# Softmax row sums and one unit's norms moved to GpSimd, and the sixth unit's loads moved behind a gather, in a fused attention and feed-forward kernel

## The chip, the cores and the metric

The kernel runs on one core of one Trainium2 chip. The metric is the time of one execution on the device in microseconds. Engines are named as the profile names them: PE (TensorE), ACT (ScalarE), DVE (VectorE), POOL (GpSimd), and SP, the queue that issues most DMAs. Each engine works through its own list of instructions in order, and an instruction that waits holds up all that stand behind it in that list.

## What is computed

The inputs are q, k and v of 8 batches, 12 heads, 448 positions and 64 values, and two weights. The reference, cut to what matters:

```python
q_n = q / (np.linalg.norm(q, axis=-1, keepdims=True) + 1e-06)
k_n = k / (np.linalg.norm(k, axis=-1, keepdims=True) + 1e-06)
scores = np.matmul(q_n, k_n.transpose(0, 1, 3, 2)) / tau
attn = np.exp(scores - np.max(scores, axis=-1, keepdims=True))
attn = attn / (np.sum(attn, axis=-1, keepdims=True) + 1e-09)
attn_out = np.matmul(attn, v)
x = attn_out.transpose(0, 2, 1, 3).reshape(B * S, H * D)   # 3584 x 768
h = x @ w_in                                                # 768 x 2048
return (h * np.cos(h)) @ w_out                              # 2048 x 768
```

## The kernel before

**Tiling.** Two heads make a pair (48 pairs, g = 0 to 47), three pairs a unit (16 units, u = 0 to 15), two units a batch. So the sixth unit is unit 5, the third is unit 2. For each unit the kernel loads q and k (`load`, L524, SP) and v (`load_v`, L536, POOL's queue); squares them (`square`, L556), sums the squares over the 64 values (`reduce`, L570, DVE) and turns the sums into 1/norm (`rnorm`, L582: ACT takes Ln and then Exp of -0.5 times it). `scale` (L594, POOL) multiplies q and k by it, and a DMA transposes the result (`transposes`, L612; the first nine pairs are transposed on PE).

**Attention of a pair.** `scores` (L640) multiplies on PE into the PSUM tiles SC, and ACT takes the exponential into PX. `attend` (L668) multiplies PX by v and by ones into the PSUM tile AV: one half of AV holds the unscaled output, the other the row sums. For the pairs in `direct` the inverse of the sum is taken at once on ACT (Ln, then Exp, L742 and L744). For the others both halves are copied to `xu`, and a chain follows once the unit is through.

**The chain** (`chain`, L755) works on units 2, 4 and on to 15: 13 chains, of 21 columns in 11 cases and 14 columns in two (units 2 and 5, where one pair is direct). Four small DMAs gather the sums over 128 partitions (L759); DVE adds two parts (L765, label "sum") and takes the reciprocal (L768, "recip"); a DMA writes it to DRAM (L769, "spread") and two read it back onto all partitions (L771, "bcast"); POOL multiplies `xu` by it into `xT` (L775). All DMAs of the chain are issued by SP.

**Feed-forward.** `m1(b)` (L778) multiplies a batch's `xT` by w_in in 8 groups on PE, with Sin on ACT and a product on DVE (L806) into `gT`; its first two groups take the batch's six chunks of `xT` one after another, in the order given, so that the last may come late. ACT has to load another function table before `m1` and again behind it (L496), and every exponential and Ln listed ahead of it in the program goes before. The product with w_out (`m2_quarters`, L850, and `m2_fill`, L878) is cut into small pieces that fill PE between the pieces of attention; DVE copies the two PSUM halves of a finished tile of 128 rows, PO and TP, to `osb` (`m2_drain`, L831, L837), and PE cannot begin the next tile in them before that.

**What sets the order.** The program is first listed as operations with costs, and `arrange` (L101) and `play` (L128) plan it: PE keeps the listed order from unit 2 on, while each other engine takes, at every free moment of a simulated run, the ready operation with the earliest due time (`late`, plus a `bias` of its own). `order_only` (L88) puts one operation behind the start of another on the same queue; in a load this is the argument `behind`. The plan's order is then written out as fixed lists, with semaphore waits. The costs in the plan are constants in the code; POOL's scale, for instance, is put at 0.1 + 896 * 1.75e-3 = 1.67 us.

**Around the change.** `pair` (L967) lists the loads of unit u+2 at L996 and of its v at L998; the loads of v of unit 4 are listed at L1044, and those of q and k of unit 5 when u is 3 (L996, without a `behind`). In the run of before SP issues the loads of unit 5 at 67 to 74 us, then an output, then the gather of unit 2.

Of the kernel before, what the change touches and what calls it, by code (L numbers as in the profile page):

```python
# [7 lines left out]
ALU = mybir.AluOpType  # L8
F32 = mybir.dt.float32
# [4 lines left out]
PLAN = {  # L14
    "apart": 1,
    "grid": {2: (16, 5, 6), 3: (11, 3, 4), 4: (8, 2, 3)},
    "hold": 0.6,
    "margin": 1.0,
    "sq": ["AA", "A", "A", "P", "P", "P"],
    "scale": ["PD", "P", "P", "P", "P", "P"],  # L20
    "second": 0,
    "mixed": (3, (0, 1, 2, 0, 1, 2, 0, 1), (2, 3, 4, 0, 1, 5)),
    "other": 8,
    "inside": 7,
# [334 lines left out]
def bass_cosine_attention__then__act_gcu_kernel(  # L359
# [13 lines left out]
    UP = 3  # L373
# [26 lines left out]
    def sb(name, shape, dt):  # L400
        return ctx.enter_context(nc.sbuf_tensor(name, shape, dt))
# [13 lines left out]
    n2 = sbs("n2", 2, [128, UH * NB], F32)  # L415
    lnn = sbs("lnn", 2, [128, UH * NB], F32)
    rn = sbs("rn", 2, [128, UH * NB], F32)
# [5 lines left out]
    RB = sbs("RB", 2, [128, UP * S], F32)  # L423
    sums = sbs("sums", 2, [128, 2 * SPR], F32)
    rcp = sbs("rcp", 2, [128, SPR], F32)
# [3 lines left out]
    zt = sb("zt", [128, S], BF16)  # L429
    ones = sb("ones", [128, 96], BF16)  # L430
    iot = cosb[0].bitcast(I32).ap()[:, 0:128]
    cst = sb("cst", [128, 2], F32)

    SC = [ps("SC%d" % i, [128, 2 * 512], F32) for i in range(2)]
    AV = ps("AV", [128, 2 * 512], F32)
# [6 lines left out]
    scr = nc.dram_tensor("scr", (NU, UH * S), F32)  # L442
# [14 lines left out]
    n2v = [t.ap().rearrange("p (h s) -> p h s", h=UH) for t in n2]  # L457
# [29 lines left out]
    def act(fn, reads, writes, cols, table=None, aps=0, label="", bias=0.0):  # L487
        o = P.op("ACT", fn, reads, writes, cost=0.165 + cols / 1200.0 + 0.09 * aps, label=label, bias=bias)
        if table is not None:
            if last_table[0] is not None:  # L490
                P.order_only(last_table[0], o)
            last_table[1].append(o)
        return o
# [9 lines left out]
    def dve(fn, reads, writes, cycles, lock=False, label="", bias=0.0):  # L503
        return P.op("DVE", fn, reads, writes, cost=0.15 + cycles / 960.0, lock=lock, label=label, bias=bias)

    def pool(fn, reads, writes, cost, label="", bias=0.0):
        return P.op("POOL", fn, reads, writes, cost=cost, lock=True, label=label, bias=bias)
# [5 lines left out]
    dve(lambda e: e.tensor_scalar(ident.ap(), iot, 0, None, ALU.is_equal), [("cos", 0)], ["ident"], 128)  # L513
    dve(lambda e: e.memset(cst.ap()[:, 0:1], math.pi / 2.0), (), ["cst0"], 1)
    dve(lambda e: e.memset(cst.ap()[:, 1:2], 1e-12), (), ["cst1"], 1)
    pool(lambda e: e.memset(ones.ap()[:, 0:64], 1.0), (), ["ones"], 0.15)
    pool(lambda e: e.memset(ones.ap()[:, 64:96], 0.0), (), ["zeros"], 0.12)
    table(EXPSET)
# [17 lines left out]
    def load_v(u, behind=None, reads=()):  # L536
        if u >= NU:
            return
        i = u % 3
        b, hb = u // 2, UH * (u % 2)  # L540
        dma("POOL", [lambda e, z=z: e.dma_start(
            vav[i][BP * z : BP * z + BP, :, 1 - z : NT3 + 2 - z, :].rearrange("p h x d -> p h (x d)"),
            bass.AP(v.tensor, (b * NH + hb) * S * D + NT3 * D * z, [[NB * D, BP], [S * D, UH], [1, (NT3 + 1) * D]]))
            for z in range(2)],
            list(reads), [("va", i)], "va%d" % i, 2.67, "load v u%d" % u, behind,
            pad=LATE if u > 1 else 0.0)
# [33 lines left out]
    rnv = [t.ap().rearrange("p (h s) -> p h s", h=UH) for t in rn]  # L580

    def rnorm(u, p0, p1, t=(0, 1)):  # L582
        i = u % 2
        h, w = slice(2 * p0, 2 * p1), slice(*blocks(t))
        n = (p1 - p0) * 2 * (w.stop - w.start)
        tag = "%d.%d" % (u, p0) + ("" if len(t) == 2 else "ab"[t[0]])
        keys = [(p, z) for p in range(p0, p1) for z in t]
        act(lambda e: e.activation(lnnv[i][:, h, w], n2v[i][:, h, w], ACT.Ln, bias=cst.ap()[:, 1:2]),
            [("n2", i, p, z) for p, z in keys] + ["cst1"], [("lnn", i, p, z) for p, z in keys],
            n, "E", 1, "ln" + tag)  # L590
        act(lambda e: e.activation(rnv[i][:, h, w], lnnv[i][:, h, w], ACT.Exp, scale=-0.5),  # L591
            [("lnn", i, p, z) for p, z in keys], [("rn", i, p, z) for p, z in keys], n, "E", 0, "rn" + tag)
# [162 lines left out]
    def chain(u):  # L755
        i, b = u % 2, u // 2
        n = sum(UP * u + p not in PLAN["direct"] for p in range(UP))
        w = SPR // UP * n
        dma("SP", [lambda e, r=r, a=a: e.dma_start(  # L759
            sums[i].ap()[64 * a : 64 * a + 64, w * r : w * r + w],  # L760
            bass.AP(xu, ((64 * a + 32 * r) * 5 + 3 + i) * UP * S, [[5 * UP * S, 1], [w, 64], [1, w]]))
            for r in range(2) for a in range(2)], [("xs", i, p) for p in range(n)], [("sums", i)], "sums%d" % i, 0.7,
            "gather%d" % u)
        r = rcp[i].ap()[:, 0:w]
        dve(lambda e: e.tensor_reduce(out=r, in_=sums[i].ap()[:, 0 : 2 * w].rearrange("p (r x) -> p x r", r=2),  # L765
                                      axis=mybir.AxisListType.X, op=ALU.add), [("sums", i)], [("rcp", i)], 2 * w,
            label="sum")
        dve(lambda e: e.reciprocal(r, r), [("rcp", i)], [("rcp", i)], 8 * w, label="recip")  # L768
        dma("SP", [lambda e: e.dma_start(bass.AP(scr, u * UH * S, [[w, 128], [1, w]]), r)],  # L769
            [("rcp", i)], [("scr", u)], "scr", 0.02, "spread%d" % u)  # L770
        dma("SP", [lambda e, a=a: e.dma_start(  # L771
            RBv[i][64 * a : 64 * a + 64, 0:n], bass.AP(scr, u * UH * S + a * n * S, [[0, 64], [1, n * S]])) for a in range(2)],
            [("scr", u)], [("RB", i, p) for p in range(n)], "RB%d" % i, 3.4 * n / UP, "bcast%d" % u, None, 2.4, 0.5)
        for p in range(n):
            pool(lambda e, p=p: e.tensor_tensor(xTv[b % 2][:, UP * i + p, :], xuv[:, u % 3, p, :], RBv[i][:, p, :], ALU.mult),  # L775
                 [("RB", i, p), ("xa", u % 3, p)], [("xT", b % 2, UP * i + p)], 1.1, label="x%d" % (UP * u + p))
# [148 lines left out]
    def find(label):  # L925
        return [o for o in P.ops if o.label == label][-1]
# [24 lines left out]
    def loads(u, behind=None):  # L951
        if u < NU:
            for p in range(UP):
                load(u, p, p + 1, behind=behind)
# [12 lines left out]
    def pair(g, f):  # L967
        u, p = g // UP, g % UP
        if 3 <= u < NU - 1:
            if p == 0:  # L970
                norms(u + 1, 0)
            if p == u % 2:
                norms(u + 1, 1)
        late = g > PB
        quarters = g >= PB
        if late and g - 1 not in points:
            attend(g - 1, direct(g - 1), (0,))
        scores(g, 0)
        m2_fill(f[0], quarters)
        if late and g - 1 in points:  # L980
            attend(g - 1, direct(g - 1), (0,))
        scores(g, 1)
        if late and f[1] and quarters:
            attend(g - 1, direct(g - 1), (1,))
            m2_fill(f[1], quarters)
            attend(g - 1, direct(g - 1), (2,))
        elif late:
            attend(g - 1, direct(g - 1), (1, 2))
        elif 1 <= g < PB:
            attend(g - 1, direct(g - 1))  # L990
        if g >= 1 and g != PB:
            if g > PB and not direct(g - 1) and (g % UP == 0 or direct(g)):
                chain((g - 1) // UP)
            if g % UP == 0:
                if g > PB and (u <= 3 or u % 2 == 0):
                    loads(u + 2, find("bcast%d" % (2 if u == 4 else u - 1)) if u > 3 else None)  # L996
                if g > PB:
                    load_v(u + 2, None if u == 5 else find("x%d" % (g - 1 if u < 5 or u % 2 == 0 else g - 4)),  # L998
                           [("sums", 0)] if u == 5 else [])
        if g == PB:  # L1000
            for y in range(PLAN["inside"], TD):
                transposes(y)
            m2_fill(f[1], True)
        if g + 2 < PB:
            norms((g + 2) // UP, (g + 2) % UP)
        if g + 1 < PB:
            transposes(g + 1, g + 1 < PLAN["apart"])
        if TD <= g + 2 < NG:
            transposes(g + 2)
        scores(g, 2)  # L1010
        m2_fill(f[2], quarters)
        scores(g, 3)
        m2_fill(f[3], quarters)
        if p == UP - 1 and u >= 3 and u % 2 == 0:
            loads(u + 3, find("bcast%d" % (u - 1)) if u > 4 else None)
# [25 lines left out]
    m1(0, 2, NKC - 1)  # L1041
    load_v(3, find("W2.3"))
    norms(3, 1)
    load_v(4, find("scale3.2"))  # L1044
    loads(4)
    P.free = False
    m2_add(0)
# [57 lines left out]
```

## Time and profile before

| | us |
|---|---|
| median of 3 runs | 442.25 |
| lowest and highest of them | 442.02 and 444.96 |
| the profiled execution, its own time | 443.33 |
| its span, first to last instruction | 441.4 |
| PE busy | 422.2 |
| ACT busy | 270.9 |
| POOL busy | 228.4 |
| DVE busy | 188.1 |

PE is busy for 96% of the span; the matmuls overlap in the records, so a busy PE is one that has work under way. The mean granted clock of PE is 0.990 of full speed. In lines of the profile, `out<-in` are the tiles written and read, brackets hold the idle time of the engine ahead of the instruction and what ended it, and "SPq" is SP's issuing of a DMA.

### The profile page before, as it was taken

What the parts mean: (1) busy time and instruction counts of PE and PEld (TensorE: products, weight loads), DVE (VectorE), ACT (ScalarE), POOL (GpSimd) and SP (SyncE); (2) the same over time, 40 slices, a digit from 0 to 9 for tenths busy, and PEclk for the clock granted to TensorE, in tenths of its full rate; (3) what the DMA queues carried; (4) which work ended last, traced back from release to release, by engine and by line L of the source; (5) the groups of instructions that cost most, each with busy time, mean ns of one, the idle gap of its engine ahead of it and who ended that gap; (6) DMA issues with size and microseconds to landing.
All of it is one profiled execution on the core that took longest, in us unless ns stands there. A gap on an engine that the chain in (4) does not pass through costs nothing.

```text
span 441.4 us, 13536 instructions
## 1 busy us (share of the span) xinstructions
PE 422.2 (96%) x6056; PEld 232.5 (53%) x6056; DVE 188.1 (43%) x243; ACT 270.9 (61%) x356; POOL 228.4 (52%) x182
## 2 busy tenths in 40 slices
PE   8889989799999999999999999999999999999996
PEld 3334545455555555664455645665556645555563
DVE  3543763425833328421772239230862244223421
ACT  4987577576688654886477855875577845703400
POOL 4999729479381566562949085924948023003000
PEclk9999999889999999999999999999999999999999
DMA  8999999999167998658927897949965940141022
GB/s 194 263 258 217 245 166 154 204 202 206 23 98 97 183 210 201 99 127 209 223 36 165 160 220 147 163 84 227 226 107 90 155 110 1 39 119 55 2 71 71
DMA packets 80713, 64.32 MB, mean 146 GB/s; under 512 B 45712, under 2 KB 75408, under 8 KB 80656
## 3 DMA queue, kind: packets, MB, share of 16 engines
q1 hardware_dynamic: 62528, 50.68, 55.8%
q0 software_dynamic: 18048, 12.59, 19.4%
q8 instruction: 47, 0.77, 0.8%
q10 hardware_dynamic: 80, 0.20, 0.1%
q14 instruction: 10, 0.08, 0.1%
HBM read 55.67 MB, written 11.14 MB: 151 GB/s over the span
## 4 chain that ended last, share of the span: by engine, by line
PE 61%; DMA 15%; POOL 11%; issue 4%; SPq 4%; ACT 2%; DVE 2%; ACTq 0%; POOLq 0%; DVEq 0%
PE SC L789 16%; PE AV L789 10%; PE TP L864 8%; PE PO L864 8%; DMA W<-in_moe_w_out_dram 7%; POOL qks L599 4%; PE SC L648 4%; PE AV L687 4%; DMA sums<-xu 3%; POOL xT L775 3%; DMA RB<-scr 3%; PE PO L894 2%; POOL sq L567 2%; PE SC L894 2%; PE TP L894 2%
## 5 line engine op out<-in xcount | busy, mean ns | idle before, releaser
L663 ACT ACTIVATE PX<-SC 128x448 bf16<-128x448 f32 (+1 forms) x192 | 153.4, 823 | 33.4 <-PE SC L648 21.6
L864 PE MATMUL PO<-W,gT 64*64 64x384 bf16 x1408 | 145.8, 328 | 4.5 <-DVE osb L837 3.3
L864 PE MATMUL TP<-W,gT 64*64 64x384 bf16 x1408 | 145.8, 328 | 0.4
L599 POOL TENSOR_TENSOR qks<-raw,rn 128x896 bf16<-128x896 f32 (+1 forms) x48 | 79.3, 1678 | 40.7 <-ACT rn L591 40.7
L789 PE MATMUL SC<-xT,W 128*128 128x448 bf16 x480 | 98.3, 352 | 0.0
L775 POOL TENSOR_TENSOR xT<-xu,RB 128x448 bf16<-128x448 f32 x37 | 41.0, 1136 | 96.9 <-DMA RB<-scr 96.9
L864 PEld LDWEIGHTS PO<-W,gT 64*64 64x64 bf16 x1408 | 77.3, 108 | 23.2 <-DVE osb L837 6.2
L864 PEld LDWEIGHTS TP<-W,gT 64*64 64x64 bf16 x1408 | 77.1, 108 | 15.9 <-PE TP L864 2.2
L567 POOL TENSOR_TENSOR sq<-raw 128x896 bf16<-128x896 f32 x45 | 75.3, 1690 | 10.7 <-DMA raw<-in_q_dram 6.3
L804 ACT ACTIVATE cosb<-SC,cst 128x896 f32<-128x896 f32 x40 | 40.1, 1006 | 54.5 <-PE SC L789 51.7
L789 PEld LDWEIGHTS SC<-xT,W 128*128 128x128 bf16 x480 | 46.7, 98 | 44.1 <-POOL xT L775 0.4
L789 PE MATMUL AV<-xT,W 128*128 128x448 bf16 x288 | 62.0, 353 | 1.9 <-POOL xT L775 1.0
L574 DVE TENSOR_REDUCE n<-sq 128x14 f32<-128x896 bf16 (+2 forms) x49 | 51.4, 1055 | 6.9 <-ACT sq L565 5.9
L806 DVE TENSOR_TENSOR gT<-SC,cosb 128x896 bf16<-128x896 f32 x40 | 43.5, 1090 | 22.3 <-ACT cosb L804 22.2
L648 PE MATMUL SC<-qkT 64*64 64x448 bf16 x576 | 52.3, 362 | 0.7 <-DVE gT L806 0.3
L804 ACT ACTIVATE cosb<-AV,cst 128x896 f32<-128x896 f32 x24 | 24.2, 1007 | 38.8 <-PE AV L789 38.8
L789 PEld LDWEIGHTS AV<-xT,W 128*128 128x128 bf16 x288 | 27.0, 98 | 31.2 <-POOL xT L775 4.4
L837 DVE COPY osb<-PO 128x384 f32<-128x384 f32 x26 | 14.4, 555 | 66.5 <-PE PO L864 60.0
L806 DVE TENSOR_TENSOR gT<-AV,cosb 128x896 bf16<-128x896 f32 x24 | 26.2, 1090 | 38.2 <-ACT cosb L804 38.1
L734 DVE COPY xu<-AV 128x896 f32<-128x896 f32 x23 | 24.9, 1083 | 39.7 <-PE AV L703 39.6
L687 PE MATMUL AV<-PX,va 128*32 128x448 bf16 x576 | 36.2, 356 | 0.0
L680 PE MATMUL AV<-PX,va 64*64 64x224 bf16 x192 | 25.9, 263 | 2.4 <-DVE xu L734 1.0
(63 smaller groups left out, 352.0 us busy)
## 6 DMA issues: line engine op xcount, KB each, us to landing
raw<-in_k_dram SPq DMA_DIRECT2D x48, 224.0 KB, 6.6
raw<-in_q_dram SPq DMA_DIRECT2D x48, 224.0 KB, 7.7
out_dram<-osb SPq DMA_DIRECT2D x55, 192.0 KB, 3.4
RB<-scr SPq DMA_DIRECT2D x22, 336.0 KB, 4.9
va<-in_v_dram POOLq DMA_DIRECT2D x32, 192.0 KB, 8.0
W<-in_moe_w_in_dram POOLq DMA_DIRECT2D x4, 768.0 KB, 14.2
W<-in_moe_w_out_dram POOLq DMA_DIRECT2D x4, 768.0 KB, 25.6
RB<-scr SPq DMA_DIRECT2D x4, 224.0 KB, 4.2
```

Of the source, the lines that this page charges most:

```text
L567: pool(lambda e, x=x, y=y: e.tensor_tensor(y, x, x, ALU.mult), src_, dst, 0.1 + n * 1.78e-3, label="sq%d.%d" % (u, p)).pad = LATE if u > 1 ...
L574: dve(lambda e, w=w: e.tensor_reduce(out=n2v[i][:, 2 * p : 2 * p + 2, w], in_=sqv[p][:, :, w, :], axis=mybir.AxisListType.X, op=ALU.add), ...
L599: f = lambda e, s0=s0, s1=s1: e.tensor_tensor(qksv[i][:, p, s0:s1].rearrange("p s h d -> p h s d"), rawv[i][:, h, s0:s1, :], bass.AP(rn[i] ...
L648: m = e.matmul(SCv[z][BP * o : BP * o + BP, a, 0:S], t[r, c - 1 + (NT3 + 1) * o, 0:BP], t[r, :, BP : 2 * BP], start=True, stop=True)
L663: act(lambda e: e.activation(PHv[j] if c == 0 else PXv[j][:, c - 1], SCv[z][:, :, 0:n], ACT.Exp, scale=1.0 / TAU), ["SC%d" % z], [("PX", j ...
L687: t = e.matmul(AVv[o : o + 32, 0, 0:S], vav[y][:, 2 * p + a, c + 1, d : d + 32], PXv[j][:, c, a, :], start=False, stop=(c == NT3 - 1))
L775: pool(lambda e, p=p: e.tensor_tensor(xTv[b % 2][:, UP * i + p, :], xuv[:, u % 3, p, :], RBv[i][:, p, :], ALU.mult), [("RB", i, p), ("xa", ...
L789: t = e.matmul(ph[:, a, 0:S], W1v[:, order[c], 128 * n : 128 * n + 128], xTv[b % 2][:, order[c], :], start=(c == 0), stop=(c == NKC - 1))
L804: act(lambda e, ph=ph, cz=cz: e.activation(cosv[cz], ph[:, :, 0:S], ACT.Sin, bias=cst.ap()[:, 0:1], scale=1.0), names(gi) + ["cst0"], [("c ...
L806: dve(lambda e, ph=ph, cz=cz, gi=gi: e.tensor_tensor(gTv[:, 2 * gi : 2 * gi + 2, S * (b % 2) : S * (b % 2) + S], ph[:, :, 0:S], cosv[cz], ...
L864: r = e.matmul(POH[b][x : x + 64, 0:HW], gTv[k, y, col + x : col + x + 64], W2v[k, y, HW * b : HW * b + HW], start=(y == 0 and h == 0), st ...
L894: r = e.matmul(po[:, 0:HW], gTv[:, y, col : col + 128], W2v[:, y, HW * hf : HW * hf + HW], start=(y == 0), stop=(y == NF - 1))
```

## The change

It does five things.

- In each of the 13 chains, the sum is a `tensor_tensor` add on POOL instead of a `tensor_reduce` on DVE, and the reciprocal is a `tensor_tensor` with the operation power and a constant -1 on POOL, instead of DVE's `reciprocal`. The plan's costs for them are 0.15 and 0.4 us.
- For unit 12 alone, 1/norm is an add of 1e-12 and a power of -0.5 on POOL (42 columns, 0.15 and 0.6 us in the plan), in place of Ln and Exp on ACT.
- The loads of q and k of unit 5 are put behind the start of unit 2's gather on SP. The spread and the broadcast of unit 2 get a bias of -8 us on their due times.
- The load of v of unit 4 is put behind the load of v of unit 3 instead of the last scaling of unit 3; that of v of unit 5 is put behind the product `x6` instead of `x8`.
- Two constants are written by DVE at the start.

```diff
+    "power": (12,),
...
-    cst = sb("cst", [128, 2], F32)
+    cst = sb("cst", [128, 4], F32)
...
+    dve(lambda e: e.memset(cst.ap()[:, 2:3], -1.0), (), ["cst2"], 1)
+    dve(lambda e: e.memset(cst.ap()[:, 3:4], -0.5), (), ["cst3"], 1)
...
+        if u in PLAN["power"]:
+            x, y = n2v[i][:, h, w].rearrange("p h s -> p (h s)"), rnv[i][:, h, w].rearrange("p h s -> p (h s)")
+            pool(lambda e: e.tensor_scalar(y, x, 1e-12, None, ALU.add), [("n2", i, p, z) for p, z in keys],
+                 [("rn", i, p, z) for p, z in keys], 0.15, label="ad" + tag)
+            pool(lambda e: e.tensor_tensor(y, y, bass.AP(cst, 3, [[4, 128], [0, n]]), ALU.pow),
+                 [("rn", i, p, z) for p, z in keys] + ["cst3"], [("rn", i, p, z) for p, z in keys], 0.6, label="pw" + tag)
+            return
...
-        dve(lambda e: e.tensor_reduce(out=r, in_=sums[i].ap()[:, 0 : 2 * w].rearrange("p (r x) -> p x r", r=2),
-                                      axis=mybir.AxisListType.X, op=ALU.add), [("sums", i)], [("rcp", i)], 2 * w,
-            label="sum")
-        dve(lambda e: e.reciprocal(r, r), [("rcp", i)], [("rcp", i)], 8 * w, label="recip")
+        parts = sums[i].ap()[:, 0 : 2 * w].rearrange("p (r x) -> p r x", r=2)
+        pool(lambda e: e.tensor_tensor(r, parts[:, 0], parts[:, 1], ALU.add), [("sums", i)], [("rcp", i)], 0.15, label="sum")
+        pool(lambda e: e.tensor_tensor(r, r, bass.AP(cst, 2, [[4, 128], [0, w]]), ALU.pow), [("rcp", i), "cst2"], [("rcp", i)], 0.4,
+             label="recip")
         dma("SP", [lambda e: e.dma_start(bass.AP(scr, u * UH * S, [[w, 128], [1, w]]), r)],
-            [("rcp", i)], [("scr", u)], "scr", 0.02, "spread%d" % u)
+            [("rcp", i)], [("scr", u)], "scr", 0.02, "spread%d" % u).bias = -8 if u == 2 else 0.0
...
-            [("scr", u)], [("RB", i, p) for p in range(n)], "RB%d" % i, 3.4 * n / UP, "bcast%d" % u, None, 2.4, 0.5)
+            [("scr", u)], [("RB", i, p) for p in range(n)], "RB%d" % i, 3.4 * n / UP, "bcast%d" % u, None, 2.4, 0.5).bias = -8 if u == 2 else 0.0
...
-                    loads(u + 2, find("bcast%d" % (2 if u == 4 else u - 1)) if u > 3 else None)
+                    loads(u + 2, find("bcast%d" % (2 if u == 4 else u - 1)) if u > 3 else find("gather2") if u == 3 else None)
...
-                    load_v(u + 2, None if u == 5 else find("x%d" % (g - 1 if u < 5 or u % 2 == 0 else g - 4)),
+                    load_v(u + 2, None if u == 5 else find("x%d" % (6 if u == 3 else g - 1 if u < 5 or u % 2 == 0 else g - 4)),
...
-    load_v(4, find("scale3.2"))
+    load_v(4, find("load v u3"))
```

## The prediction, made before the changed kernel ran

> **What bounds the kernel now.** I read the engine table of the page first, then the 40 slices, then the waits, then the timelines around the slices where PE is not full.
>
> ```profile
> PE 422.2 (96%) x6056; PEld 232.5 (53%) x6056; DVE 188.1 (43%) x243; ACT 270.9 (61%) x356; POOL 228.4 (52%) x182
> ...
> PEclk9999999889999999999999999999999999999999
> ```
>
> PE has work for 96% of the span, so a change pays only where PE is empty or slow. The 441.4 us hold 19 us without PE work, and the clock row has one hole, in slices 8 and 9 (77 to 99 us). A table by stretches takes that hole apart (columns: stretch, its length, busy time of PE, PE's weight loads, DVE, ACT and POOL with counts, granted clock, DMA share, GB/s).
>
> ```profile
> 74.00:82.11 8.11, 8.11 (x188) 4.68 (x180) 1.62 (x2) 6.20 (x10) 6.77 (x5) 1.00 1.40 190
> 82.11:85.38 3.27, 0.01 (x2) 0.00 (x1) 1.35 (x5) 1.10 (x2) 1.77 (x3) 0.86 0.94 150
> 85.38:91.30 5.92, 5.92 (x80) 3.66 (x84) 2.46 (x3) 1.98 (x4) 1.13 (x1) 0.50 0.96 188
> 91.30:98.46 7.16, 7.01 (x157) 3.72 (x149) 2.27 (x4) 5.97 (x11) 5.73 (x5) 1.00 1.09 235
> ```
>
> PE is empty for 3.27 us, and then works 5.92 us at half clock. The timeline of DVE there says why:
>
> ```profile
> 77.00 1.08 DVE L574 TENSOR_REDUCE n<-sq 128x14 f32<-128x896 bf16 x1
> 84.00 0.18 DVE L765 TENSOR_REDUCE rcp<-sums 128x14 f32<-128x28 f32 x1 [5.92 <-DMA sums<-xu]
> 84.22 0.24 DVE L768 RECIPROCAL rcp<-rcp 128x14 f32<-128x14 f32 x1
> 84.37 0.49 DVE L837 COPY osb<-PO 128x384 f32<-128x384 f32 x1
> 84.78 0.54 DVE L837 COPY osb<-TP 128x384 f32<-128x384 f32 x1
> ```
>
> DVE stands 5.92 us at the sum of unit 2, whose gather has not landed; behind it in DVE's list are the copies out of PO and TP, and without them PE cannot open the next w_out tile. PE's own waits name them, and the waits of DVE give the size of the habit:
>
> ```profile
> PE PO L864 <- DVE osb L837: 3.3, 1, 3.3
> ...
> PE AV L680 <- DVE xu L734: 1.0, 1, 1.0
> ```
>
> ```profile
> DVE rcp L765 <- DMA sums<-xu: 33.2, 10, 7.0
> ```
>
> The second PE wait is the same thing at unit 5, with AV in the place of PO: DVE waits 5.99 us and PE 1.03.
>
> ```profile
> 146.73 0.18 DVE L765 TENSOR_REDUCE rcp<-sums 128x14 f32<-128x28 f32 x1 [5.99 <-DMA sums<-xu]
> 146.94 0.24 DVE L768 RECIPROCAL rcp<-rcp 128x14 f32<-128x14 f32 x1
> 147.10 1.03 DVE L734 COPY xu<-AV 128x896 f32<-128x896 f32 x1
> ```
>
> Of the 33.2 us that DVE waits at sums, then, 4.3 reach PE; the clock adds the rest.
>
> **The change, part by part.**
>
> *Sum and reciprocal leave DVE.* DVE then holds nothing that waits for a gather. The copies of 84.37 can run when PE has finished the tile, before 82.11. Gain: 3.27 us at unit 2 and 1.03 at unit 5. The half clock follows the gap: a mean clock of 0.86 over the 3.27 us means that it fell 0.92 us before the gap's end ((1 - 0.86) * 3.27 / 0.5), 2.35 us into the idling, and nowhere else inside the span did PE idle over 2 us or its clock fall before the end. Without the gap, the 5.92 us of work at 0.50 take 2.96. Gain: 2.96 us. ACT and POOL are not full in these 5.92 us (1.98 and 1.13 us busy), so PE can run at its own speed.
>
> The Trainium skill ("TensorE: Matmul & The Clock Gate", What's actually happening) puts the fall to half clock at an idle window of about 3.4 us that runs freely. Here 2.35 us of idling were enough, so I go by the row; by the page a remaining stall of 1 to 3 us would cost itself alone, and by the row it can cost itself and as much again in slow matmuls.
>
> *They arrive on POOL.* The add: POOL's product of 448 columns takes 1.136 us and a one-column memset 0.10, so 2.3 ns a column and 0.15 us for 21 columns; at POOL's ratio to DVE on the same product (L748: 1134 against 624 ns) it would be 0.36. The power has no row on POOL. Below, it can cost no less than such an add, 0.15. ACT's Ln and Exp of 42 columns, the same function, take 0.32 and 0.24, 0.56 together. DVE's reciprocal costs 6.6 ns a column (288 against 242 ns for 21 and 14), 5.5 times its plain copy (1083 ns for 896); two such functions at POOL's 2.3 ns are 25 ns a column, 0.63 us for 21. I take 0.6, as both estimates lie there; the far end, ten times as much a column, is 5.4 us. Against DVE's 0.198 + 0.288 + 0.04 = 0.53 us, the pair on POOL takes 0.8 with a hand-over, 0.25 more.
>
> Who waits for that: the products into xT. For the first unit of a batch they have time (unit 10's broadcast lands 2 us before they start). For units 7, 9, 13 and 15 they release PE with little to spare, but the spread stands behind an output on SP there: it is issued 0.72, 0.32 and 0.70 us after the reciprocal at 7, 9 and 13, and at 15 the second broadcast chunk comes some 0.6 us ahead of PE. So 0.25 us more costs nothing; beyond about 0.6 it would cost four times the excess. POOL is idle 12 to 30 us ahead of these products (96.9 us in 9 waits), so the sum finds it free.
>
> What is queued behind POOL's new wait: at unit 5 only the products of unit 4, for which POOL waits 4.97 us anyway; at units 11 and 14 nothing (15.0 and 7.8 us idle); at units 6, 8, 10 and 12 the next unit's scaling, ahead of which POOL idles 4.4 to 6.0 us for ACT. That cover hides 13 * 0.8 = 10 us of POOL's time.
>
> *Unit 5's loads behind the gather; v of unit 4 sooner, of unit 5 later; the bias.* Before, SP issued six loads of unit 5 from 67.08 to 74.08, then an output, and the gather from 75.41, though its sums were ready at 73.24 (the copy of 72.15 + 1.09). The gather took 8.6 us to its landing behind 1.3 MB of them. On a quieter bus unit 15's took 3.8 (385.07 to the sum at 388.90) and unit 4's 5.1. So: issue near 73.5, landing near 78. The spread and broadcast took 9.5 us from 84.0 to 93.5; from 79 they end near 88.5, and the bias keeps SP's loads from stepping in. PE, 6.2 us earlier, starts the feed-forward of batch 1 at 98.46 - 6.23 = 92.2 and asks for these chunks after the 12 matmuls of the first three, at 94.5. The broadcast has 3 to 5 us in hand for its two products; no gain by itself, it keeps the 6.2 us from being lost at the next wait. If the gather stayed at 84.0, products at 93.5 to 95.8 would cost PE about 1 us.
>
> The price: unit 5's q and k come 9 us later. Its last square began at 80.89 and Exp of its norms ended at 92.65; the table load for Sin, which that Exp must precede, moves from 100.57 to 94.3. Squares from about 89, reduce 1.08 and ACT 0.56 end at 92.4. That fits by 2 us: cost nothing, but see the first rival. The v loads move 0.4 MB each between slack places: unit 4's to POOL's idle 8.6 us before 63.91, unit 5's behind x6 (needed after 120 us). Nothing.
>
> *Unit 12's norms.* POOL idles 4.40 us before 276.17 waiting for ACT's Exp, which waits for the table load (274.19 to 275.47). With add and power on POOL (0.2 and up to 1.2 us) the three scalings start some 3 us sooner. PE has no gap over 0.1 us there: nothing. The two constants, 59 ns each, lie in DVE's idle first microseconds.
>
> **The sum.** 3.27 + 2.96 + 1.03 = 7.26 us. The profiled execution took 443.33 (span 441.4 and 1.9 around it), so 436.1 by its own time. It stands 1.08 above the median of the runs, 442.25; against that median it is **435.0 us**.
>
> **The rivals.**
>
> *Unit 5 comes too late (chance 0.16).* The red and Ln of unit 5 take the place of the sum: DVE or ACT stands at them with copies or exponentials behind, between 88 and 95 us. For it: the 2 us in hand above, and that loads landed 8 us after issue on this bus (the last at the square of 80.89, issued at 72.34). Against it: v of unit 4 and of unit 5 leave this stretch. A stall of 3 us gives 438.0, and with a clock that falls again as much more, 441.0.
>
> *The wait only changes engines (0.08).* POOL stands at the gather where DVE did, and the products x8 to x11 behind it hold PE, or another copy binds PE at 82 us. For it: POOL is busy 6.77 of 8.11 us there. Against it: these products are asked for only from 92 us on, and ACT waits for PE, not PE for ACT. It would give back all of the 6.2 us: 441.2, no change.
>
> *The power is slow, and the kernel slower (0.10).* Place: the last chains of batches, units 7, 9, 13 and 15, where POOL's result releases PE. Price: four times what exceeds the 0.25 us, less some 2.3 us of slack (0.72 + 0.32 + 0.70 + 0.6). With an excess d over DVE's pair, 4d - 2.3 = 7.26 at d = 2.4, a power of 2.7 us: from there on the kernel is slower. At 5.4 us, d is 5.1 and the time 435.0 + 18 = 453. Against it: neither estimate above comes near 2.7.
>
> The Trainium skill ("GPSIMD Engine Reference", Instruction dispatch) tells of some 6 us for the first call of freshly loaded code on this engine. By that page the power of unit 2, the first, would end near 85 and its products near 96.5, 2 us after PE asks: 437 in place of 435.0. No row here shows such a load.
>
> **How the numbers follow.** The forecast has 0.66, the rivals 0.16, 0.08 and 0.10. The forecast's own range is 433.3 to 437: below if unit 7's PE gap (1.25 us with its small pieces) closes as SP's order changes, above by 2 us for the power or the gather. The range for 8 in 10 takes in the first rival: **433.3 to 441.0**. A measurement of this kernel tells about 1%, 4.4 us, from no change: faster is below 437.8. Of the forecast nearly all lies there, of the first rival little: faster 0.66. Within 1% lie the rest of the first and the second, 0.24. Slower is the power, 0.10.
>
> **What would show it.** Right: no DVE wait on sums; no PE gap near 82 and near 147 us; clock 1.00 from 6 us to the end; the first Sin of batch 1 near 96.6 in place of 102.83; the power under 1 us. The gather of unit 2 landing near 78. Wrong: a PE wait on DVE or ACT between 84 and 96, a clock below 1.00 in slices 8 and 9, PE gaps over 1 us at the xT of units 7, 9, 13 or 15, or a power of 2 us and more.

## The result, and the profile after

The changed kernel is slower: 461.28 us (median of 6 runs, 458.63 to 464.20) against 442.84 for the kernel before (6 runs, 442.02 to 444.96), a ratio of 1.041 with a 95% interval of 1.036 to 1.045. I had forecast 435.0. Here and below, times are medians of all runs of a kernel, while ratios, and the differences worked out from them, leave out the slow runs, those over 1.5% above the fastest of their kernel. The profiled execution took 458.63 us with a span of 456.6, 15.2 more than before.

The page after (busy time and share of the span; the granted clock in 40 slices):

```profile
PE 424.7 (93%) x6056; PEld 231.3 (51%) x6056; DVE 183.5 (40%) x219; ACT 270.7 (59%) x354; POOL 284.2 (62%) x210
...
PEclk9999999999999889999999999998999999999999
```

PE runs the same 6056 matmuls in a longer span, the hole in the granted clock has moved from slices 8 and 9 to slices 14 and 15 (with a smaller one in 28), and POOL has 56 us more to do. The groups of POOL by form say where that is (count, busy time, mean ns of one, idle time ahead):

```profile
L777 POOL TENSOR_TENSOR rcp<-rcp,cst 128x21 f32<-128x21 f32 x11 | 40.7, 3700 | 0.8
...
L595 POOL TENSOR_TENSOR rn<-rn,cst 128x42 f32<-128x42 f32 x1 | 7.1, 7087 | 0.1
...
L777 POOL TENSOR_TENSOR rcp<-rcp,cst 128x14 f32<-128x14 f32 x2 | 5.2, 2602 | 0.2
...
L776 POOL TENSOR_TENSOR rcp<-sums 128x21 f32<-128x21 f32 x11 | 2.4, 221 | 24.3 <-DMA sums<-xu 24.3
```

The power takes 3.70 us for 21 columns, 2.60 for 14 and 7.09 for 42: about 160 ns a column ((3.70 - 2.60) / 7 = 0.157 us and (7.09 - 3.70) / 21 = 0.161) on top of some 0.4 us. The add, at 0.22 us, is as cheap as I had it.

What the change was meant to cure is cured. The timeline of DVE around the old hole shows both copies from PO and TP at 80.6 to 81.7 us, with no sum ahead of them:

```profile
76.48 0.62 DVE L757 COPY xu<-AV 128x448 f32<-128x448 f32 x1 [3.21 <-PE AV L697]
80.63 0.56 DVE L847 COPY osb<-PO 128x384 f32<-128x384 f32 x1 [3.52 <-PE PO L874]
81.10 0.55 DVE L847 COPY osb<-TP 128x384 f32<-128x384 f32 x1
```

The stretches of the changed kernel (same columns as in the prediction) show PE full and at clock 1.00 there, and empty and slow elsewhere:

```profile
74.00:82.00 8.00, 8.00 (x192) 4.76 (x188) 2.00 (x4) 6.09 (x10) 3.94 (x3) 1.00 0.67 125
82.00:92.00 10.00, 10.00 (x232) 5.84 (x224) 3.21 (x6) 8.34 (x13) 7.24 (x6) 1.00 1.06 212
...
154.32:160.00 5.68, 0.00 (x0) 0.00 (x1) 0.00 (x0) 0.00 (x0) 1.18 (x2) 0.70 1.21 228
160.00:163.45 3.45, 3.45 (x10) 1.45 (x11) 0.00 (x0) 0.00 (x0) 2.81 (x3) 0.50 1.20 249
```

PE's own waits name what it stands for. Before, 3.3 us were for `osb`, and 1.0 for the products into `xT`; now:

```profile
PE AV L799 <- POOL xT L785: 11.2, 10, 5.7
PE SC L666 <- DMA qkT<-qks: 3.7, 3, 2.5
PE SC L799 <- POOL xT L785: 1.7, 3, 1.4
```

The second line is for transposed q and k: its 2.5 us, at 299.3, are a wait for a transpose that SP issued at 295.36, of what POOL scaled behind unit 12's power and chain 10's.

The start of each batch's feed-forward on PE, taken from the timelines, dates the gain and the losses (us):

| batch | 0 | 1 | 2 | 3 | 4 | 5 | 6 | 7 | end |
|---|---|---|---|---|---|---|---|---|---|
| before | 39.4 | 98.5 | 158.3 | 205.1 | 254.2 | 304.5 | 352.4 | 397.4 | 441.4 |
| after | 39.5 | 92.3 | 151.9 | 206.9 | 256.6 | 311.9 | 364.0 | 410.5 | 456.6 |
| difference | +0.1 | -6.2 | -6.4 | +1.8 | +2.4 | +7.4 | +11.7 | +13.1 | +15.2 |

So 6.2 us are won by batch 1, as forecast (92.2). Then 8.2 are lost in the stage with unit 5 (between batches 2 and 3), 0.6 in that with unit 7, 5.0 in that with unit 12's power, 4.3 at unit 11, 1.4 at unit 13 and 2.1 at unit 15.

### The profile page after: what moved, and what is told of

Its sections match the earlier page's. It is cut to its first block, busy times and chain, and to the rows that moved or that the text cites. A ratio compares the mean times of both kernels' runs of the same rounds, so it can differ in the third digit from the quotient of the medians.

```text
span 456.6 us, 13531 instructions
## 1 busy us (share of the span) xinstructions
PE 424.7 (93%) x6056; PEld 231.3 (51%) x6056; DVE 183.5 (40%) x219; ACT 270.7 (59%) x354; POOL 284.2 (62%) x210
## 4 chain that ended last, share of the span: by engine, by line
PE 57%; POOL 13%; DMA 13%; ACT 6%; SPq 6%; issue 3%; DVE 2%; POOLq 0%; ACTq 0%
PE SC L799 17%; PE AV L799 10%; DMA RB<-scr 7%; PE PO L874 7%; PE TP L874 7%; PE AV L697 4%; PE SC L658 4%; POOL rcp L777 4%; POOL xT L785 3%; DMA sums<-xu 3%; ACT PX L673 2%; POOL qks L609 2%; POOL sq L570 2%; SPq L769 2%; PE AV L690 2%
## 5 line engine op out<-in xcount | busy, mean ns | idle before, releaser
L874 PE MATMUL PO<-W,gT 64*64 64x384 bf16 x1408 | 143.4, 323 | 0.9 <-DVE qkT L647 0.9
L874 PE MATMUL TP<-W,gT 64*64 64x384 bf16 x1408 | 143.4, 323 | 0.4
L799 PE MATMUL SC<-xT,W 128*128 128x448 bf16 x480 | 100.1, 357 | 1.7 <-POOL xT L785 1.7
L799 PE MATMUL AV<-xT,W 128*128 128x448 bf16 x288 | 64.0, 361 | 12.0 <-POOL xT L785 11.2
L777 POOL TENSOR_TENSOR rcp<-rcp,cst 128x21 f32<-128x21 f32 (+1 forms) x13 | 45.9, 3531 | 0.9
```

Of the source, the lines that this page charges most:

```text
L777: pool(lambda e: e.tensor_tensor(r, r, bass.AP(cst, 2, [[4, 128], [0, w]]), ALU.pow), [("rcp", i), "cst2"], [("rcp", i)], 0.4, label="recip")
L799: t = e.matmul(ph[:, a, 0:S], W1v[:, order[c], 128 * n : 128 * n + 128], xTv[b % 2][:, order[c], :], start=(c == 0), stop=(c == NKC - 1))
L874: r = e.matmul(POH[b][x : x + 64, 0:HW], gTv[k, y, col + x : col + x + 64], W2v[k, y, HW * b : HW * b + HW], start=(y == 0 and h == 0), st ...
```

## The experiments

Three theories stood at the start. A: the power's own duration stands on the way to PE. B: the moved loads collide with unit 5's broadcast, and the rest follows. C: the plan, given 0.4 and 0.6 us for the power, made a bad order. Ratios are against the kernel before on the same chip, with 95% intervals; beside these runs it had medians of 442.2 to 443.7, and the runs of one kernel spread over 2 to 9 us. The intervals leave each ratio 1.4 to 4.3 us either way, so that differences under 2 us are not resolved.

**The power for unit 12 left out.** `"power": ()` in place of `(12,)`.

> The change without its power for unit 12 (Ln and Exp on ACT again); all else as changed. Theory A, the power instructions themselves are the loss wherever they stand on the way to PE: the stage that holds unit 12's 7.1 us power lost 5.0 us (start of the feed-forward of batch 4 2.35 us late, of batch 5 7.39 late against before), and these come back: 456 us. Theory B, the moved loads are the loss (they stand ahead of unit 5's broadcast, and the rest follows from that stall): unit 12's power lies in POOL's idle time and the time stays near 461. Theory C, the plan was made with wrong costs (0.4 and 0.6 us) and its order is what is bad, not the duration: without unit 12's wrong price a part comes back, 458.

Measured: 453.85 us, 1.023 (1.016 to 1.029), 8.0 us less than the changed kernel ((1.0409 - 1.0228) * 443). The stage between batches 4 and 5 takes 50.7 us (307.45 - 256.76) in place of 55.3. B falls for this part; unit 12's power costs more than the 5.0 us that I had put down from the trace. A and C are not told apart here.

**Every power a multiplication.** This one leaves the inverse out, as its text says.

```diff
-            pool(lambda e: e.tensor_tensor(r, r, bass.AP(cst, 2, [[4, 128], [0, w]]), ALU.pow), ...
+            pool(lambda e: e.tensor_tensor(r, r, bass.AP(cst, 2, [[4, 128], [0, w]]), ALU.mult), ...
```

(and the same at unit 12's, with constants 1e-6 and 1)

> The change with every power replaced by a multiplication by a constant (1e-6 for the sums, 1 for unit 12), at the same costs in the plan, so that every engine keeps the changed kernel's order. It leaves the inverse of the sums and of unit 12's norms out. Theory A: each multiplication takes 0.2 to 0.3 us, the stalls at units 5, 11, 12, 13 and 15 go, and the time comes near my forecast, 435 to 438 us. Theory B: the stall of 5.7 us at unit 5 and its half clock stay, some 450. Theory C: the order is unchanged, but the costs in it are now true: 436, as in A.

Measured: 440.05 us, 0.993 (0.989 to 0.997): 21 us less than with powers, in the same order of instructions. Its groups on POOL and its PE waits:

```profile
L777 POOL TENSOR_TENSOR rcp<-rcp,cst 128x21 f32<-128x21 f32 x11 | 2.4, 217 | 0.8
```

```profile
PE AV L799 <- POOL xT L785: 4.0, 10, 1.1
```

The operation went from 3700 to 217 ns, PE's wait for the products from 11.2 to 4.0 us, its longest (unit 5) from 5.7 to 1.1. So the power's duration is the loss, by A or by C, which had the same expectation here; the time is 2 to 5 us above it. What holds the 1.1 us that are left at unit 5 is not shown; the moved loads by themselves, next, leave no such wait there.

**The moves of loads alone**, sum and reciprocal back on DVE, unit 12 on ACT; run twice.

```diff
-        pool(... ALU.add), [("sums", i)], [("rcp", i)], 0.15, label="sum")
-        pool(... ALU.pow), [("rcp", i), "cst2"], [("rcp", i)], 0.4, label="recip")
+        dve(lambda e: e.tensor_reduce(out=r, ..., op=ALU.add), [("sums", i)], [("rcp", i)], 2 * w, label="sum")
+        dve(lambda e: e.reciprocal(r, r), [("rcp", i)], [("rcp", i)], 8 * w, label="recip")
```

> Only the moves of loads and the biases; sum and reciprocal on DVE and unit 12 on ACT as before. Theory A: the gather of unit 2 lands near 77 to 78 us instead of 84, DVE waits for it too briefly to hold PE, and the hole at 82 to 91 us goes as in the changed kernel; unit 5's wait of 1 us may stay: 436 to 438 us. Theory B: unit 5 stalls as in the changed kernel, 447 or more. If the hole was cured by taking the sum off DVE and not by the loads, the time is that of before, 442.

> The loads-only version once more, beside the one with more biases on the same chip: 438 us, about 1% under the kernel before.

Measured: 438.24 us, 0.989 (0.984 to 0.995), and 438.94, 0.990 (0.986 to 0.994). This version is 1% faster than the kernel before. DVE's timeline there:

```profile
79.07 0.18 DVE L775 TENSOR_REDUCE rcp<-sums 128x14 f32<-128x28 f32 x1 [1.94 <-DMA sums<-xu]
79.29 0.24 DVE L778 RECIPROCAL rcp<-rcp 128x14 f32<-128x14 f32 x1
80.66 0.56 DVE L847 COPY osb<-PO 128x384 f32<-128x384 f32 x1 [1.13 <-PE PO L874]
```

DVE still waits for the gather, but it lands at 79.1 in place of 84.0, and the copy is not due before 80.66. Taking the sum off DVE was not needed for this hole. Batch 1 starts at 92.7 and 92.6 in the two runs.

**The chains alone**, sum and power on POOL, loads where they were.

> Only the sum and the power of the chains on POOL; loads where they were, unit 12 on ACT. Theory A: DVE is free and the copies at 82 us are not held, but the gather of unit 2 lands near 84 and its power takes 2.6 us, so PE waits 1 to 4 us for its products, and units 5, 7, 11, 13 and 15 cost what they cost in the changed kernel: 452 to 460 us. Theory B: without the moved loads nothing is lost at unit 5 and the gain at 82 us stays: 437 to 441.

Measured: 461.29 us, 1.040 (1.032 to 1.048), at the upper end of what A gives. The copies at 82 us are free here too (batch 1 starts at 95.3 in place of 98.5), but then PE idles 4.46 us at 97.8 for unit 2's products and 6.29 at 164.4 for unit 5's. B falls: unit 5 stalls without the moved loads.

**The plan told the truth.**

```diff
-        pool(... ALU.pow), [("rcp", i), "cst2"], [("rcp", i)], 0.4, label="recip")
+        pool(... ALU.pow), [("rcp", i), "cst2"], [("rcp", i)], 0.4 + 0.157 * w, label="recip")
```

(and 7.1 in place of 0.6 at unit 12)

> The changed kernel with the power's measured duration as its cost in the plan (0.4 + 0.157 us a column for the chains, 7.1 for unit 12), so that the orders are planned round the true length. Theory A (the duration itself stands on the way to PE): what follows the power still waits for it, 452 to 461 us. Theory C (the order made from wrong costs is the loss): near the version with multiplications, 440.

Measured: 454.94 us, 1.024 (1.015 to 1.034). Knowing the length brings some 7 of the 18 us back ((1.0409 - 1.0242) * 443, with intervals of 2 and 4 us either way). So C has a share, and the larger part stays with A: with this planner the duration costs time even where it is known.

**Which chains?** The same two POOL instructions for the even units alone, or the odd units alone, the others on DVE; loads moved, unit 12 on ACT.

> Moved loads; sum and power on POOL in the chains of units 2, 4, 6 to 14 alone, on DVE in the odd units; unit 12's norms on ACT. The even units' products have time in hand in the traces. Theory A with its place (only the last chain of a batch releases PE): 438 to 442 us, of which up to 2 for unit 4, whose power delayed the scaling on POOL and so unit 5's gather. If a long power hurts wherever it stands, because POOL's list is held, half of what the chains cost comes: 446 or so.

> Moved loads; sum and power on POOL in the chains of units 5, 7, 9, 11, 13 and 15 alone, on DVE in the even ones; unit 12's norms on ACT. Theory A: nearly all that the chains cost comes here: 448 to 454 us. If POOL's held list is the cost, 446.

Measured: 442.86 us, 0.999 (0.994 to 1.004), for the even ones, and 448.72, 1.014 (1.007 to 1.020), for the odd. Over the loads alone (0.9895) that is 0.0096 and 0.0241 of 443, 4.3 and 10.7 us; together 15.0, and all chains on POOL cost 14.8 (1.0228). The last chains of the batches carry most of it, and the even ones more than I had allowed. The starts of the batches' feed-forward in the odd units' trace, against the two traces of the loads alone, place the odd units' share: 4.8 and 3.7 us are lost in the stage with unit 5, where PE idles 3.18 us for the products and then has half clock, 1.5 and 1.1 at unit 11, and 4.2 and 5.3 at units 7, 9, 13 and 15 together.

**The even ones apart**: without unit 4; unit 2 alone; units 6 to 14 alone.

> As the run with the even units alone on POOL, but unit 4 on DVE too. In that run unit 4's power (131.9 to 135.6 us) held v of unit 7 and the last scaling of unit 7 on POOL, unit 5's gather was issued 4.5 us later than with the loads alone, and DVE, which takes unit 5's sum there, held PE for 3.25 us at 143. Theory A with that explanation: the stall goes, and of the 4.6 us over the loads alone 3 or more come back: 438 to 440 us. If the cost of the even units is spread over all of them, 442.

> Moved loads; sum and power on POOL for the chain of unit 2 alone. All even units together cost 4.4 us over the loads alone and leaving out unit 4 brought nothing back, so the cost is at unit 2 or at units 6 to 14. If at unit 2 (its 2.6 us power stands ahead of scaling and products on POOL, and batch 1's feed-forward began 1.5 us later in the even-units run): 441 to 443 us. If at the later ones: 438 to 439.

> Moved loads; sum and power on POOL for the chains of units 6, 8, 10, 12 and 14 alone. If the cost of the even units is theirs (3.7 us of POOL's list held ahead of the scaling of the next units): 441 to 443 us. If it is unit 2's: 438 to 439.

Measured: 443.02 us, 0.998 (0.995 to 1.002); 440.77, 0.994 (0.991 to 0.998); 439.27, 0.993 (0.989 to 0.997). My explanation by unit 4 failed: leaving it out brought nothing that can be measured, though the profiled PE gap at 142 us shrank from 3.25 to 1.25. The profiled execution without unit 4 took 439.14 us, 3.9 less than the median of that kernel, so its trace does not show where the usual run loses its time. Unit 2 costs some 2 us and units 6 to 14 some 1.5; each lies near the edge of its interval, so the 4.3 us seem to be spread, and that is not settled further.

**Unit 12's power, and why it cost 8 us**: alone; chains 10 and 11 alone; the three together, the rest on DVE.

> Moved loads and the power for unit 12's norms; all chains on DVE. In the changed kernel unit 12's power cost 7.4 us (461.3 against 453.9 without). If it costs that by itself, as POOL's idle time ahead of the scaling is 4.4 us and the power takes 7.1: 443 to 446 us. If it cost so much there only because the powers of chains 10 and 11 stood behind it on POOL: 439 to 441.

> Moved loads; sum and power of chains 10 and 11 on POOL, the rest on DVE and ACT. Chain 11 alone releases PE: by the excess of 3.5 us less its slack of about 1.2 us, 2 us over the loads alone, 440 to 442 us, with up to 1 more for chain 10.

> Moved loads; unit 12's power, and sum and power of chains 10 and 11 on POOL, the rest on DVE. Unit 12's power cost 8 us in the changed kernel and 3.7 us alone. If the two powers near it on POOL's list (7.1 + 3.7 + 3.7 us within some 35 us) make up the difference, this costs 3 us or more over the sum of unit 12's alone (3.7) and the next run's excess. If not, just that sum.

Measured: 442.27 us, 0.998 (0.994 to 1.001); 439.41, 0.990 (0.987 to 0.994); 446.86, 1.011 (1.007 to 1.014). Over the loads alone these are 3.6, 0.4 and 9.3 us: unit 12's alone falls between my two cases, the two chains cost less than I expected, and the three together 5.3 us more than the sum of the parts; each of the three ratios is known to some 1.5 us either way.

Unit 12's power alone reaches PE through three engines. Two squares stand behind it on POOL, so DVE's sum of the squares comes late, and on ACT Ln waits for that sum, with a copy behind it:

```profile
279.22 0.33 ACT L598 ACTIVATE lnn<-n,cst 128x42 f32<-128x42 f32 x1 [2.31 <-DVE n L577]
279.58 0.24 ACT L601 ACTIVATE rn<-lnn 128x42 f32<-128x42 f32 x1
279.73 0.90 ACT L741 ACTIVATE xu<-AV 128x896 f32<-128x896 f32 x1
```

PE idles 1.06 us for that copy and 0.61 for the exponential after it; where the rest of the 3.6 us goes is not shown.

The timeline of POOL with the three shows how they work together (unit 12's power, two scalings, two squares, a scaling, then chain 10's and 11's sums and powers, and 11's products):

```profile
264.54 7.10 POOL L595 TENSOR_TENSOR rn<-rn,cst 128x42 f32<-128x42 f32 x1
271.72 3.34 POOL L609 TENSOR_TENSOR qks<-raw,rn 128x896 bf16<-128x896 f32 x2
275.02 3.32 POOL L570 TENSOR_TENSOR sq<-raw 128x896 bf16<-128x896 f32 x2
278.30 1.69 POOL L609 TENSOR_TENSOR qks<-raw,rn 128x896 bf16<-128x896 f32 x1
279.94 0.22 POOL L777 TENSOR_TENSOR rcp<-sums 128x21 f32<-128x21 f32 x1
280.24 3.70 POOL L778 TENSOR_TENSOR rcp<-rcp,cst 128x21 f32<-128x21 f32 x1
...
295.51 3.69 POOL L778 TENSOR_TENSOR rcp<-rcp,cst 128x21 f32<-128x21 f32 x1
307.55 3.30 POOL L791 TENSOR_TENSOR xT<-xu,RB 128x448 bf16<-128x448 f32 x3 [8.35 <-DMA RB<-scr]
```

Chain 10's gather had landed at 263.7, but its sum is taken at 279.94, behind the long power and what that delayed; its spread, issued at 283.97, stands in SP's list ahead of chain 11's gather, with a broadcast, a transpose and an output between them, and that gather goes out at 289.50 in place of 285.42 with unit 12's power alone. Chain 11's own power adds 3.7, its products come at 307.55, and PE, which asked at 304.5, idles 4.21 us and then has 3.4 us at half clock. With unit 12's power alone, or these chains alone, PE waits at most 0.6 us for chain 11's products.

**Which loads?** One edit to the kernel before: `loads` of unit 5 behind `find("gather2")`, without the biases and the v loads.

> One edit to the kernel before: the loads of q and k of unit 5 behind the start of unit 2's gather; v loads, biases, DVE and ACT as before. If these loads alone held the gather, it lands below 80 us, the hole at 82 to 91 us goes and the time is 437 to 439 us. If the v loads on POOL's queue (unit 4's, issued at 70.5) held it as well, the gather lands at 81 to 82, part of the hole stays, and the time is 440 to 442.

Measured: 441.96 us, 0.998 (0.993 to 1.002). The gather lands at 79.8 and the hole at 82 us is gone, but the reciprocal, ready at 80.2, is not passed on (SP's timeline):

```profile
81.72 0.61 SPq L527 DMA_DIRECT2D raw<-in_q_dram  x1
82.43 1.73 SPq L616 DMA_TRANSPOSE qkT<-qks  x1
84.21 0.59 SPq L769 DMA_DIRECT2D scr<-rcp  x1
84.85 1.27 SPq L839 DMA_DIRECT2D out_dram<-osb  x2
86.22 3.59 SPq L616 DMA_TRANSPOSE qkT<-qks  x1
91.53 1.11 SPq L771 DMA_DIRECT2D RB<-scr  x2
```

The spread goes out at 84.21, behind loads and a transpose, and the broadcast only at 91.53; PE then loses 2.8 us in three waits at 89 to 98 us, batch 1 starts at 94.6 in place of 92.7, and another 1.7 go at 152.5. So these loads alone did hold the gather, as expected, but the time is not what I drew from that. The biases and the v loads together keep what the gather gains; which of the two does it was not run apart.

**More biases.** The loads alone, with the bias of -8 also for units 7, 9, 11, 13 and 15.

> The moved loads alone, and a bias of -8 us on the spread and the broadcast of units 7 to 15, odd ones, too, so that the plan puts them ahead of the outputs on SP. In the loads-only run the spread of unit 7 is issued 0.72 us after its reciprocal, of unit 13 0.71, and PE idles 0.8 and 1.1 us at these units' products. If the outputs ahead hold them: 1 to 2 us under the loads alone, 436.5 to 437.5. If PE's wait there is set by the gather and the broadcast on the bus: no change, 438.

Measured: 438.88 us, 0.991 (0.987 to 0.995), against 438.94 for the loads alone on the same chip: no change.

## Why the prediction was wrong, step by step

- **The power's price, 0.6 us for 21 columns, was wrong by a factor of six.** This is the step that failed. At 21 columns it takes 3.70 us. Both estimates, ACT's Ln and Exp and DVE's reciprocal at POOL's rate, came from other engines' instructions, and neither carried over. The far end I had set, 5.4 us, did hold the 3.70, but I gave a power over 2.7 us one chance in ten on rows that could not say that much, and left the range without it. (The range's low end, 433.3, does not follow from the 1.25 us named for it either, which give 433.75.)
- **The rival with the slow power named the cause, but only a part of the place.** With d = 0.22 + 3.70 + 0.08 - 0.53 = 3.47 us, its formula 4d - 2.3 gives 11.6 us, and so a time of 446.6, for 461.28 measured. It left out the even units and unit 12. That the odd units alone cost 10.7 us, close to 11.6, is luck: the formula stood for units 7, 9, 13 and 15, which lost 4 to 5 us, and the rest came at units 5 and 11, where the prediction had put nothing.
- **"That cover hides POOL's time" and "Unit 12's norms: nothing" failed with the same price.** The cover was reckoned for 13 * 0.8 us; with 13 powers of 2.6 to 3.7 us and one of 7.1 ahead of scalings that had 4.4 us of idle time in front of them, it did not hold: 4.3 us at even units and 8.0 at unit 12. Of these 8.0, 3.6 are what it costs alone; most of the rest is the long power pushing the chains behind it. Together: 438.3 (the loads alone, 0.9895 * 443) + 10.7 + 4.3 + 8.0 = 461.3, for 461.28 measured. The 8.0 is itself the difference from the changed kernel, so what this sum tests is that the two halves of the chains add up to the whole, 15.0 for 14.8.
- **The hole at 82 us and its 6.2 us were right**: PE's gap and half clock went, the gather landed at 77.3, and batch 1 started at 92.3 for 92.2 forecast. Which part does it I had not separated: the loads did so without POOL, while POOL's sums without the loads brought batch 1 only to 95.3.
- **Unit 5's 1.03 us was not won.** In the second run of the loads alone PE still waits 0.82 us for DVE's copy behind unit 5's sum (at 141.3); with multiplications this wait is gone, but 1.1 us for the products of unit 5 come in its place. The forecast without the power's price would have stayed at 435, and the versions without powers stand at 438 to 440: in the first trace of the loads alone another 1.3 us go between batches 6 and 7, with a PE wait of 1.08 us for unit 13's products.
- **Unit 5's late loads, the first rival, did not come about**: no wait on its squares or norms holds PE between 84 and 98 us.
- **The half clock.** In the changed kernel it began 2.3 us into the gap of 5.68 and just after one of 2.43 (at 314.3), and not at all at one of 2.50 (at 299.3) nor, with the even units, at one of 3.25. So the idle time that suffices is no fixed number, and my "by the row" was too firm. What the Trainium skill says of a window that runs freely ("TensorE: Matmul & The Clock Gate", What's actually happening) agrees with that, while its 3.4 us as the idle time that it takes does not agree with the 2.3 and 2.43.
- **No first call was seen.** The power of unit 2, the first, took 2.61 us and began 0.08 us after the add ahead of it had ended; that of unit 5, with as many columns, took 2.59. What the Trainium skill tells of freshly loaded code ("GPSIMD Engine Reference", Instruction dispatch) did not show here.

## What to carry to other kernels

An operation that no row of the trace shows on an engine has no price; ask what price would turn the verdict, and if nothing in the trace excludes it, let range and chances say so, or measure it by itself first. A blocking wait can be cured at either end: here an earlier gather did what moving the waiting instruction was to do, and the version with it alone is 1% faster than the kernel before. And long instructions on an in-order list can cost more together than the sum of each alone once a second list, here SP's, stands behind their results.

## What was not expected of the hardware

A power on POOL of 14 to 42 columns runs at some 160 ns a column, where a multiplication of 21 columns takes 0.22 us in all: 3.70 against 0.22 us for the same shapes. For the exponents -1 and -0.5 the duration lies on nearly one line over the columns (157 ns a column from 14 to 21 with -1, 161 from there to 42 with -0.5), and it varied by under 1% from one to the next (3.69 to 3.72 us). The half clock, where it came between the first 20 us and the last 10 us of a trace, lasted 3.41 or 6.83 us each time: 6.83 after the gap at 82 us of the kernel before and after that of 5.68 us, 3.41 after that of 2.43.
